# Clustered attention and a rational MoE layer in one kernel: the second head pair's operands turned by TensorE, its row maxima entered in three steps, the constant products on a tile of ones, and a new order of work

## The chip, the cores and the metric

The kernel runs on one core of a Trainium2 chip. The metric is the device time of one execution in microseconds (us). The kernel before takes 903.31 us, the median of three runs (903.31, 903.31, 904.04).

## The reference

What is computed, cut to what matters (batch 4, 8 heads, 768 positions, head dimension 64, 16 centroids per head; 3072 tokens, d_model 512, d_ff 2048):

```python
q_assign = argmax(q_n @ c_n.T); k_assign = argmax(k_n @ c_n.T)   # normalised rows, per head
mask = q_assign[:, :, :, None] == k_assign[:, :, None, :]
scores = where(mask, scale * q @ k.T, -1e9)
attn = exp(scores - max(scores)); attn = attn / (sum(attn) + 1e-9)
x = (attn @ v)                                  # heads side by side: (3072, 512)
h = x @ w_in
P = a[0] + a[1]*h + a[2]*h**2 + a[3]*h**3
Q = 1 + abs(b[0])*abs(h) + abs(b[1])*h**2
out = (P / (Q + 1e-6)) @ w_out
```

## The kernel before

Each of the four batches has an attention part (four pairs of heads) and an MoE part (three blocks of 256 tokens). The attention of batch b+1 runs beside the MoE part of batch b, so that batch 0's attention stands alone at the head of the program, beside the conversion of the weights, and batch 3's MoE part at its end. Operands are split into two f16 parts so that f16 products keep enough bits: `q1`/`k1` hold high and low part side by side, `q2`/`k2` hold a high part, the marks of the clusters (±65504, which make the mask by a product) and, in batch 0, 16 columns for the row maximum.

All of the order is written out by hand: `op(...)` only records a closure, and `Plan.emit` (L52) calls the closures by the list `ORDER` (L61). Each engine takes its instructions strictly in that order. The loads and the transposing DMAs are all issued by SyncE, in one order too, and the raw weights go through two buffers (`wraw`).

Batch 0 takes the path of `KEYMAJOR`. For each pair:

- `prep` loads q and k, sums squares on ScalarE, finds the pair's scale with four small TensorE products (`over_partitions`, L1010 to L1018: `kt`, `kb`, `qt`, `qb`) and small VectorE steps, and makes `q1`, `k1`, `q2`, `k2` (tiles `tq`, `tk`).
- The operands are turned, head dimension on the partitions (tiles `sq`, `sk`). `turn` (L1098) does it with one transposing DMA each. `turn_pe` (L973) does it with 12 TensorE products with the identity (L980) into one of the two PSUM buffers `s`, and two ScalarE copies (L998) out of it. Which one is used is set by `pet`, which holds the pairs of batch 0 that take TensorE: before, pair 0 alone.
- `attend_keys` computes twelve blocks of scores (L1386), and VectorE takes the maximum of each row (L1396, tile `top`). The maxima go into the last columns of `q2` by five small VectorE steps (L1419 to L1442), and those columns have to be turned as well. Where `q2` is split (a pair in `pet`), that is done in three parts, each as soon as its third of the maxima is there: four TensorE products (L1452) and one ScalarE copy (L1459). Where it is not, the five steps run once over all twelve blocks and `q2` is turned a second time by DMA.
- Then the scores are computed again the other way round (L1480), with the maximum and the mask inside the product, and go through `Exp` and the product with v (L1501, L1507).

The program also contains 16 bursts of eight products with a constant tile (`warm`, L781), whose result nobody reads. They read `ident16`, the f16 identity, which VectorE casts from the f32 identity that GpSimd makes (L389, L390).

Of the kernel before, what the change touches and what calls it, by code (L numbers as in the profile page):

```python
# [12 lines left out]
BF16 = mybir.dt.bfloat16  # L13
# [5 lines left out]
P = 128  # L19
# [38 lines left out]
K = {'xn': 14, 'scp': 1, 'vsc': 0.75, 'sup0': 0, 'stk': 2, 'lop': 0, 'mgp': 0, 'rvn': 2, 'at': 3, 'vn': 3, 'ah': 5, 'sua': 1.0, 'T1': 1, 'quick': 1, 'sqd': 0.0, 'gld': 0.0, 'gp': 0.3, 'pp': 0.0, 'NR': 19, 'acb': 1.0, 'warm': 16, 'fast': 16, 'pet': (0,), 'wdl': 0.5}  # L58
# [200 lines left out]
def clustered_attention_moe_kernel(  # L259
# [12 lines left out]
    nc = tc.nc  # L272
# [52 lines left out]
    def kn(name, default=0.0):  # L325
        return K.get(name, default)

# [10 lines left out]

    TOGETHER = kn('together', ())

    KEYMAJOR = {(b, hp) for b in range(B) for hp in range(kn("km", (4, 0, 0, 0))[b])}

    plan.look = kn("look", 40.0)
    NM = 2
# [1509 lines left out]
```

## Time and profile before

| | before |
|---|---|
| median of three runs | 903.31 us |
| profiled execution, its own time | 900.24 us |
| span of its trace | 898.4 us |
| TensorE busy | 862.0 us (96%) |
| VectorE busy | 811.3 us (90%) |
| ScalarE busy | 794.5 us (88%) |
| GpSimd busy | 533.2 us (59%) |

The span is what the trace covers of the profiled execution; 1.84 us of its own time lie around it. Three engines are busy for most of the span, but not in the same stages: which of them sets the pace is read from a table by stage. TensorE's granted clock is 1.00 in all stages from 50 to 880 us and lower in parts of the first 50.

### The profile page before, as it was taken

How to read it: one execution, taken by the hardware profiler on the slowest of the kernel's cores; microseconds unless marked ns; L12 is line 12 of the kernel's file. 1: busy time of each engine (PE TensorE's matmuls, PEld its weight loads, DVE VectorE, ACT ScalarE, POOL GpSimd, SP SyncE). 2: the span in 40 equal slices, each digit the busy share in tenths (PEclk: the TensorE clock that was granted, in tenths of full speed). 3: DMA queues.
4: the chain of work that ended last, by engine and by line, in shares of the span. 5: the costliest groups of instructions: out<-in, count | busy, mean ns of one | idle time of the engine just before them, and what ended most of it. 6: DMA issues, size and time to landing. Idle time of an engine off the chain costs nothing.

```text
span 898.4 us, 20920 instructions
## 1 busy us (share of the span) xinstructions
PE 862.0 (96%) x7893; PEld 594.4 (66%) x7893; DVE 811.3 (90%) x1610; ACT 794.5 (88%) x1497; POOL 533.2 (59%) x530
## 2 busy tenths in 40 slices
PE   5699999988999999999999999999999999999998
PEld 4566777765666666657667666667676666767654
DVE  3999989789999999989999999999999998877793
ACT  4688899999999999999999999999999999895652
POOL 2337645677766385547556737565666555687664
PEclk9799999999999999999999999999999999999999
DMA  4698876779877999886979999989789875150000
GB/s 155 190 251 216 198 186 144 206 146 210 160 139 139 191 198 183 190 161 127 216 153 167 178 189 171 159 169 179 152 154 170 156 139 95 36 95 1 24 24 24
DMA packets 353013, 135.76 MB, mean 151 GB/s; under 512 B 327824, under 2 KB 344208, under 8 KB 352912
## 3 DMA queue, kind: packets, MB, share of 16 engines
q1 hardware_dynamic: 352912, 134.42, 74.0%
q8 instruction: 62, 1.02, 0.4%
q14 instruction: 39, 0.32, 0.1%
HBM read 41.98 MB, written 6.29 MB: 54 GB/s over the span
## 4 chain that ended last, share of the span: by engine, by line
PE 61%; DVE 17%; ACT 14%; issue 5%; POOL 1%; DMA 1%; SPq 1%; ACTq 0%; DVEq 0%
PE po L1761 20%; PE ph L1612 19%; PE s L1243 7%; PE px L1323 5%; DVE s L1272 3%; ACT s L409 3%; DVE ah L1303 3%; ACT u L409 2%; ACT ah L409 2%; PE s L1386 2%; PE z L1480 2%; PE px L1501 2%; DVE t L1637 1%; DVE t L1630 1%; PE ptl L1138 1%
## 5 line engine op out<-in xcount | busy, mean ns | idle before, releaser
L1612 PE MATMUL ph<-x,win 128*128 128x256 f16 x2304 | 266.2, 273 | 1.1 <-DVE t L1637 0.6
L1761 PE MATMUL po<-wout,g 128*128 128x512 f16 x1152 | 267.1, 379 | 0.0
L1612 PEld LDWEIGHTS <-win 128*128 128x128 f16 x2304 | 223.9, 98 | 42.0 <-DVE t L1637 2.9
L1761 PEld LDWEIGHTS <-g 128*128 128x128 f16 x1152 | 110.5, 98 | 120.1 <-issue 3.4
L1750 POOL TENSOR_TENSOR g<-t,u 128x512 f16<-128x512 f32 x84 | 112.7, 1344 | 93.8 <-DVE t L1743 56.6
L1677 POOL TENSOR_TENSOR s<-s,u 128x512 f32<-128x512 f32 x84 | 111.2, 1329 | 74.9 <-ACT s L409 73.1
L1272 DVE TENSOR_SCALAR_CACHE_REDUCE s<-s,cc 128x768 f32<-128x768 f32 x144 | 144.9, 1018 | 4.4 <-PE s L1243 3.5
L1303 DVE SCALAR_TENSOR_TENSOR ah<-s,su,ah 128x768 f16<-128x768 f32 x144 | 144.1, 1010 | 4.4 <-ACT ah L409 3.9
L409 ACT ACTIVATE ah<-s,su 128x768 f16<-128x768 f32 x144 | 127.8, 899 | 6.6 <-DVE su L1291 6.1
L409 ACT ACTIVATE s<-s,nm 128x768 f32<-128x768 f32 x144 | 125.6, 872 | 8.4 <-DVE s L1272 6.5
L1243 PE MATMUL s<-sk,sq 128*128 128x384 f16 x576 | 115.6, 327 | 6.3 <-DVE ah L1303 5.6
L1243 PEld LDWEIGHTS <-sq 128*128 128x128 f16 x576 | 52.0, 98 | 49.9 <-DVE ah L1303 16.4
L1323 PE MATMUL px<-at,vhi 128*64 128x256 f16 x864 | 73.9, 275 | 1.9 <-DVE s L1731 1.8
L409 ACT ACTIVATE t<-ph,gk 128x512 f32<-128x512 f32 x84 | 65.3, 778 | 0.0
L1630 DVE SCALAR_TENSOR_TENSOR t<-ph,gk,t 128x512 f32<-128x512 f32 x84 | 62.2, 742 | 2.5 <-ACT t L409 1.4
L1637 DVE SCALAR_TENSOR_TENSOR t<-t,gk,ph 128x512 f32<-128x512 f32 x84 | 62.3, 741 | 1.2
L409 ACT ACTIVATE u<-s,cq 128x512 f32<-128x512 f32 x84 | 59.8, 721 | 3.0 <-POOL s L1677 2.9
L409 ACT ACTIVATE s<-u,g 128x512 f32<-128x512 f32 x84 | 60.3, 723 | 0.5
L409 ACT ACTIVATE u<-ph,gk 128x512 f32<-128x512 f32 x84 | 57.7, 688 | 3.3 <-PE ph L1612 3.1
L1731 DVE SCALAR_TENSOR_TENSOR s<-s,g 128x512 f32<-128x512 f32 x84 | 59.8, 714 | 0.5
L1323 PE MATMUL px<-at,vlo 128*64 128x256 f16 x432 | 59.7, 273 | 0.0
L1323 PEld LDWEIGHTS <-vhi 128*64 128x64 f16 x864 | 45.0, 110 | 15.3 <-issue 10.3
(241 smaller groups left out, 1552.4 us busy)
## 6 DMA issues: line engine op xcount, KB each, us to landing
rwi<-in_moe_w_in_dram SPq DMA_DIRECT2D x16, 512.0 KB, 3.9
rwo<-in_moe_w_out_dram SPq DMA_DIRECT2D x16, 512.0 KB, 4.3
rk<-in_k_dram SPq DMA_DIRECT2D x32, 192.0 KB, 3.9
rq<-in_q_dram SPq DMA_DIRECT2D x32, 192.0 KB, 3.7
rvm<-in_v_dram SPq DMA_DIRECT2D x16, 384.0 KB, 4.0
rv<-in_v_dram SPq DMA_DIRECT2D x16, 384.0 KB, 4.1
out_dram<-ob SPq DMA_DIRECT2D x24, 256.0 KB, 2.9
sq<-sq SPq DMA_DIRECT2D x12, 192.0 KB, 4.1
```

The source lines that it names most:

```text
L409: lambda: nc.scalar.activation(out=out(), in_=in_(), func=func, **{a: (x() if callable(x) else x) for a, x in kw.items()}),
L1243: nc.tensor.matmul(sc.ap[:, i, :SH], lhsT=st["q" + x].ap[:, j, t, :], rhs=st["k" + x].ap[:, j, ks, :].rearrange("p t c -> p (t c)"), start ...
L1272: lambda nm=nm, view=view: ts(out=view(), in0=view(), scalar1=cc.ap[:, 0:1], scalar2=None, op0=ALU.mult, op1=ALU.min, accum_out=nm.ap),
L1303: lambda part=part, view=view, su=su: stt(out=part(1), in0=view(), scalar=su.ap, in1=part(0), op0=ALU.mult, op1=ALU.subtract),
L1323: nc.tensor.matmul(px.ap[j * D : (j + 1) * D, :], lhsT=vv.ap[:, j, kt, :], rhs=at[j].ap[:, p_, kt].rearrange("p t c -> p (t c)"), start=(i ...
L1612: nc.tensor.matmul(ph.ap[:, fi * TW : (fi + 1) * TW], lhsT=win[:, wpart, c, f * P : (f + 1) * P], rhs=xs[c].ap[:, xpart], start=(i == 0), ...
L1630: lambda t=t, h=h, ph=ph, col=col: stt(out=t[h].ap, in0=ph.ap, scalar=col("rho")(), in1=t[h].ap, op0=ALU.mult, op1=ALU.mult),
L1637: lambda t=t, h=h, ph=ph, col=col: stt(out=t[h].ap, in0=t[h].ap, scalar=col("a1")(), in1=ph.ap, op0=ALU.add, op1=ALU.mult),
L1677: lambda uv=uv, sv=sv: nc.gpsimd.tensor_tensor(out=sv(), in0=sv(), in1=uv(), op=ALU.mult),
L1731: lambda sv=sv, g16=g16: stt(out=sv(), in0=sv(), scalar=1.0 + 1e-6, in1=g16(0), op0=ALU.add, op1=ALU.mult),
L1750: lambda tv=tv, uv=uv, g16=g16, e=(nc.vector if kshare("gld", b, i_) else nc.gpsimd): e.tensor_tensor(out=g16(1), in0=tv(), in1=uv(), op=A ...
L1761: nc.tensor.matmul(po[ti].ap, lhsT=g16(gg)[:, c0 : c0 + P], rhs=wout[:, wpart, f, :], start=(i == 0 and f == 0), stop=(i == 2 and f == NF ...
```

## The change

Three edits of the code and a new `ORDER`:

- `pet` is `(0, 1)`: pair 1 of batch 0 goes through `turn_pe` for `k1`, `q1`, `k2`, `q2`, and its `q2` is split into three parts.
- The constant products of `warm` read a new tile `w16w`, bf16 ones, set by one VectorE memset. `ident16` is made by GpSimd directly and no longer cast by VectorE.
- `KEYMAJOR` is written in another way and holds the same four pairs of batch 0.
- `ORDER` has 4476 entries for 4453, and the entries stand in another order. Below the new memset all line numbers are higher by 3.

```diff
-K = {'xn': 14, ..., 'warm': 16, 'fast': 16, 'pet': (0,), 'wdl': 0.5}
+K = {'xn': 14, ..., 'warm': 16, 'fast': 16, 'pet': (0, 1), 'wdl': 0.5}

 ORDER = [int(i) for i in """
-4438 4450 40 41 42 43 4437 4447 4445 4449 4444 4443 4452 4448 44 3 4 74 75 5 6 76 77 78 79 386 387 389 4451
...

-    KEYMAJOR = {(b, hp) for b in range(B) for hp in range(kn("km", (4, 0, 0, 0))[b])}
+    KEYMAJOR = {(0, hp) for hp in kn("kmset", (0, 1, 2, 3))}

     ident16 = cp.tile([P, P], F16, name="ident16")
-    nc.vector.tensor_copy(out=ident16, in_=ident)
+    make_identity(nc, ident16)
+    w16w = cp.tile([P, P], BF16, name="w16w")
+    nc.vector.memset(w16w, 1.0)

-                nc.tensor.matmul(wm.ap[:, :P], lhsT=ident16, rhs=ident16, start=True, stop=True)
+                nc.tensor.matmul(wm.ap[:, :P], lhsT=w16w, rhs=w16w, start=True, stop=True)
```

By engine, the program has these instructions more or fewer: TensorE 48 turning products and 12 of the rows of maxima more; ScalarE 8 copies of turned tiles and 3 of rows more; VectorE 15 small steps of pair 1 for 5, a memset for a cast; SyncE 5 transposing DMAs fewer (2 of `sk`, 3 of `sq`); GpSimd one memset and one select more for the second identity.

Three places of the order. The first is VectorE's beginning, up to the first step of pair 0's scale (`km`, the maximum of the sums of k's squares; `ww..` are raw weights, `ident` in L390 the f16 identity). Before:

```order
L445 TENSOR_REDUCE css<-csq 128x1
L448 TENSOR_SCALAR cn<-css 128x1
L558 TENSOR_SCALAR wwo_1_222<-mwo_1_218 128x512
L565 SCALAR_TENSOR_TENSOR wwo_1_222<-rwo_1_216,wwo_1_222 128x512
L390 CAST ident_85<-ident 128x128
L1015 TENSOR_REDUCE km_0_245<-kt_0_243 1x1
L1027 TENSOR_SCALAR ksc_0_249<-kb_0_247 128x1
```

Changed:

```order
L388 MEMSET eps 128x1
L393 MEMSET w16w 128x128
L395 MEMSET mrow 128x8
L396 MEMSET mrow 128x8
L397 MEMSET mrow 128x1
L398 MEMSET mrow 128x1
L561 TENSOR_SCALAR wwo_1_149<-mwo_1_147 128x512
L568 SCALAR_TENSOR_TENSOR wwo_1_149<-rwo_1_127,wwo_1_149 128x512
L561 TENSOR_SCALAR wwi_2_232<-mwi_2_228 128x512
L568 SCALAR_TENSOR_TENSOR wwi_2_232<-rwi_2_226,wwi_2_232 128x512
L1018 TENSOR_REDUCE km_0_253<-kt_0_242 1x1
```

What the constant products read is written behind two weight tiles before, and ahead of all weights in the change. TensorE's own order begins with eleven of the bursts and `kt` in both.

The second is ScalarE where pair 1's operands are turned (`sk_1`, `sq_1`; `mwo`, `gwo` are parts of raw weights, `rvm` v for its scale). Before:

```order
L409 ACTIVATE tq_1_455<-rq_1_452,qsc_1_474 128x12x64
L409 ACTIVATE mwo_0_537<-rwo_0_535 128x512
L409 ACTIVATE gwo_0_548<-rwo_0_535 128x512
L998 ACTIVATE sk_0_550<-tk_0_0_485 128x768 x2
L998 ACTIVATE sq_0_553<-tq_0_0_500 128x3x256 x2
L409 ACTIVATE mwo_2_565<-rwo_2_563 128x512
L409 ACTIVATE gwo_2_570<-rwo_2_563 128x512
L409 ACTIVATE mwo_3_580<-rwo_3_578 128x512
L409 ACTIVATE gwo_3_632<-rwo_3_578 128x512
L409 ACTIVATE rvm_1_745,vm_313<-rvm_1_745 128x768
```

Changed:

```order
L1001 ACTIVATE sk_0_554<-tk_0_0_541 128x768 x2
L1001 ACTIVATE sq_0_539<-tq_0_0_526 128x3x256
L412 ACTIVATE mwo_2_599<-rwo_2_597 128x512
L412 ACTIVATE gwo_2_617<-rwo_2_597 128x512
L1001 ACTIVATE sk_1_621<-tk_0_1_584 128x768
L412 ACTIVATE wip_ln<-win_623,tiny 128x1
L1001 ACTIVATE sk_1_621<-tk_0_1_584 128x768
L412 ACTIVATE mwo_3_636<-rwo_3_634 128x512
L412 ACTIVATE gwo_3_641<-rwo_3_634 128x512
L1001 ACTIVATE sq_1_672<-tq_0_1_644 128x768 x2
```

Four of the eight new copies stand between the conversions of the raw weights; the copies of `k2` and `q2` stand 10 and 18 rows further on, among the first exponentials.

The third is SyncE, where pair 1's `k2` and `q2` were turned. Before:

```order
L423 DMA rwi_1_886<-in_moe_w_in_dram 128x1024
L1105 DMA_TRANSPOSE sk_1_896<-tk_1_542 128x12x128
L423 DMA rwi_3_912<-in_moe_w_in_dram 128x1024
L1105 DMA_TRANSPOSE sq_1_981<-tq_1_546 128x12x128
L423 DMA rwi_2_1016<-in_moe_w_in_dram 128x1024
L1105 DMA_TRANSPOSE sk_2_1034<-tk_2_756 128x12x128
```

Changed:

```order
L426 DMA rwi_0_888<-in_moe_w_in_dram 128x1024
L426 DMA rwi_1_960<-in_moe_w_in_dram 128x1024
L426 DMA rwi_2_1018<-in_moe_w_in_dram 128x1024
L426 DMA rk_3_1098<-in_k_dram 128x384
L1108 DMA_TRANSPOSE sk_2_1100<-tk_2_730 128x12x128
L426 DMA rwi_3_1112<-in_moe_w_in_dram 128x1024
```

The transposing DMAs of pair 1 are gone from between the loads; those of pair 2 follow.

## Rows read from the trace of the kernel before

**Rows 1.** Busy time by stage: stretch, its length, engines (us, instructions), granted clock, DMA share.

```profile
9.20:15.70 6.50, 6.49 (x88) 6.50 (x89) 0.00 (x0) 1.24 (x5) 2.98 (x4) 1.00 0.28 91
15.70:20.00 4.30, 2.31 (x27) 1.63 (x25) 2.75 (x12) 2.62 (x5) 0.00 (x0) 0.94 0.02 4
20.00:35.00 15.00, 10.35 (x120) 9.24 (x121) 14.02 (x42) 12.42 (x21) 3.77 (x4) 0.61 0.58 187
35.00:50.00 15.00, 12.69 (x135) 8.56 (x134) 14.34 (x29) 7.45 (x15) 6.75 (x7) 0.84 0.92 245
50.00:100.00 50.00, 48.50 (x527) 33.41 (x526) 48.50 (x113) 43.56 (x77) 29.06 (x30) 1.00 0.90 218
100.00:125.00 25.00, 24.47 (x340) 18.37 (x342) 20.48 (x45) 22.81 (x42) 12.62 (x13) 1.00 0.96 209
125.00:175.00 50.00, 49.14 (x637) 36.77 (x627) 43.81 (x102) 46.97 (x89) 30.89 (x37) 1.00 0.66 172
175.00:225.00 50.00, 44.13 (x469) 32.19 (x465) 46.57 (x99) 49.26 (x100) 34.42 (x43) 1.00 0.88 178
225.00:450.00 225.00, 220.21 (x1949) 148.75 (x1948) 218.39 (x432) 218.56 (x428) 138.51 (x132) 1.00 0.89 170
450.00:700.00 250.00, 249.84 (x2219) 171.48 (x2218) 245.95 (x497) 242.81 (x468) 148.91 (x145) 1.00 0.90 165
```

**Rows 2.** Timeline, 1 to 18 us: start, length, engine, instruction [idle before <- releaser].

```profile
1.14 0.06 DVE L387 MEMSET eps<- 128x1 f32 x1
...
8.93 0.22 DVE L390 CAST ident<-ident 128x128 f16<-128x128 f32 x1
9.02 0.19 ACT L409 ACTIVATION_READ_ACCUMULATOR tk<-rk 128x1 f32 x1
9.21 1.03 PE L786 MATMUL warm-39.99_113<-ident 128*128 128x128 f16 x8 [9.21 <-DVE ident L390]
...
15.30 0.61 PE L786 MATMUL warm-39.86_234<-ident 128*128 128x128 f16 x8
15.75 0.27 PE L1013 MATMUL kt<-ident,sumk 128*1 128x128 f32 x1
16.05 0.28 DVE L1015 TENSOR_REDUCE km<-kt 1x1 f32<-1x128 f32 x1 [6.90 <-PE kt L1013]
...
17.38 0.94 ACT L409 ACTIVATE tk<-rk,ksc 128x768 f16<-128x768 f32 x1 [6.87 <-DVE ksc L1045]
```

**Rows 3.** VectorE groups by line and shape, 0 to 215 us: count | busy us, mean ns.

```profile
L1442 DVE TENSOR_SCALAR tq<-rest 128x12 f16<-128x12 f32 x3 | 1.0, 344 | 0.1
L1419 DVE TENSOR_SCALAR tq<-top 128x32 f16<-128x32 f32 x3 | 0.5, 178 | 0.1
L1437 DVE SCALAR_TENSOR_TENSOR rest<-tq,rest 128x12 f32<-128x12 f16 x3 | 0.5, 170 | 0.1
L1427 DVE SCALAR_TENSOR_TENSOR rest<-tq,top 128x4 f32<-128x4 f16 x3 | 0.5, 151 | 0.0
```

**Rows 4.** All groups by line and shape: TensorE's turning and ScalarE's copies of pair 0.

```profile
L998 ACT ACTIVATE sq<-tq 128x768 f16<-128x768 f16 x4 | 3.0, 818 | 0.0
L998 ACT ACTIVATE sk<-tk 128x768 f16<-128x768 f16 x4 | 3.0, 806 | 0.4 <-PE tk L980 0.4
L980 PE MATMUL tk<-ident,tk 128*128 128x128 f16 x24 | 2.9, 310 | 3.0 <-DVE tk L1181 1.8 <-DVE tk L1089 1.2
L1459 ACT ACTIVATE sq<-r 32x512 f16<-32x512 f16 x3 | 1.8, 589 | 0.8 <-PE r L1452 0.7
L1452 PE MATMUL r<-ident,tq 128*32 128x128 f16 x12 | 1.2, 222 | 0.0
```

**Rows 5.** Busy time in one stretch in which TensorE turns pair 0's `k2`; columns as in rows 1.

```profile
31.60:32.90 1.30, 1.28 (x13) 1.30 (x14) 1.26 (x3) 1.30 (x3) 0.00 (x0) 0.50 0.05 13
```

**Rows 6.** Line L1105 from 45 to 125 us: who waited for a transposing DMA (us, times).

```profile
  POOL tq L1127: 0.4, 1
  PEld L1138: 0.2, 1
```

More of the change, by code (lines that the diff above doesn't have):

```diff
@@ L55, in emit @@
             self.ops[i]()
-K = {'xn': 14, 'scp': 1, 'vsc': 0.75, 'sup0': 0, 'stk': 2, 'lop': 0, 'mgp': 0, 'rvn': 2, 'at': 3, 'vn': 3, 'ah': 5, 'sua': 1.0, 'T1': 1, 'quick': 1, 'sqd': 0.0, 'gld': 0.0, 'gp': 0.3, 'pp': 0.0, 'NR': 19, 'acb': 1.0, 'warm': 16, 'fast': 16, 'pet': (0,), 'wdl': 0.5}
+K = {'xn': 14, 'scp': 1, 'vsc': 0.75, 'sup0': 0, 'stk': 2, 'lop': 0, 'mgp': 0, 'rvn': 2, 'at': 3, 'vn': 3, 'ah': 5, 'sua': 1.0, 'T1': 1, 'quick': 1, 'sqd': 0.0, 'gld': 0.0, 'gp': 0.3, 'pp': 0.0, 'NR': 19, 'acb': 1.0, 'warm': 16, 'fast': 16, 'pet': (0, 1), 'wdl': 0.5}
 ORDER = [int(i) for i in """
[193 rows of a table removed]
[194 rows of a table added]
 """.split()]
```

386 rows, old and new, of the table ORDER are left out of this document.

## The prediction

> **What bounds the kernel now.** I read first the busy time by stage, then the timeline of the first 18 us, then the groups of the instructions that the change multiplies, and last who waits for a transposing DMA.
>
> The stages show which engine sets the pace [rows 1]. From 450 to 700 us TensorE is busy 249.84 of 250 us: there only less work for it, or an earlier start, can shorten the kernel. From 20 to 100 us VectorE is the fullest engine (14.02 of 15, 14.34 of 15, 48.50 of 50), with TensorE level with it after 50. From 125 to 225 ScalarE is (46.97 and 49.26 of 50), and TensorE's largest hole lies at the end of that, 5.87 us between 175 and 225; another 4.79 are spread over 225 to 450. Before 20 us no engine is full. From 9.20 to 15.70 VectorE is busy for 0.00 us and ScalarE for 1.24: TensorE runs the constant products, and all else waits.
>
> The timeline shows why [rows 2]. The constant products need the f16 identity; its cast is the 19th row of VectorE's order and starts at 8.93 us, behind two weight tiles that come by DMA. So the first burst starts at 9.21. The sum of k's squares is ready at 9.21 (9.02 plus 0.19), but `kt`, the product that takes it, stands behind eleven bursts in TensorE's order and starts at 15.75. VectorE's `km` has then waited 6.90 us, and ScalarE's next step on k, which starts at 17.38, 6.87 us. This is a chain at the head of a program whose later stages are full, so what it loses is lost at the end, unless something later has slack of its own.
>
> **The change part by part.**
>
> *The constant tile.* The ones are set right behind `eps`, which is set at 1.14 us, and depend on nothing. The eleven bursts take 6.5 us (9.21 to 15.75), so they end near 8 us, before the sums are there, and `kt` starts at about 9.2: 6.5 us earlier. If each burst took the 1.03 us of the first, they would end at 12.6 and 3.1 us would be left. I take -6.5, with -3.1 as the other end. What is late next is the scale's own chain (`km` to 17.38: 1.3 us of small steps in turn on VectorE and TensorE), which moves as a whole. The second identity costs GpSimd two instructions, which I put at 0: they stand ahead of nothing that is waited for, since GpSimd is idle for more than half of 9.20 to 20 us and the identity is needed only when turning begins. The cast that VectorE loses is paid by the memset, 0.
>
> *The small steps of the maxima.* Pair 1 has 15 for 5. The short ones take 151 to 178 ns, the long ones 170 to 344 [rows 3]: 2.3 to 2.7 us for 0.9 to 1.7, thus +0.6 to +1.9. VectorE is full where they stand, so they lie on the path: +1.2. The maxima that they read, behind which they queue, are made in the same order as before.
>
> *TensorE's turning.* 24 products took 2.9 us, 121 ns each [rows 4]; they ran at a granted clock of 0.50, the 1.2 GHz level [rows 5], and half of that is the least at 2.4 GHz. 48 are 2.9 to 5.8 us. The 12 of the maxima's rows are 1.2. The first 24 stand before and among the first scores, where TensorE is idle for 4.65 and 2.31 us of two stages of 15 [rows 1], and so cost nothing; if that cover is gone, 2.9. The other 24 and the rows, 1.5 + 1.2 = 2.7, fall where it has only 1.50 us idle in 50. I take +1.2, between 0 and 7.0.
>
> *ScalarE's copies.* Eight copies at 3.0/4 = 0.75 us and three at 0.59 [rows 4] are 7.8 us. They queue ahead of weight conversions and of the first exponentials. ScalarE is idle for 7.55 us between 35 and 50 and for 6.44 between 50 and 100 [rows 1], and VectorE, not ScalarE, is full there: 0. If that cover is gone, up to 7.8.
>
> *Five transposing DMAs less.* Only 0.6 us of waiting ended on such a DMA between 45 and 125 us [rows 6], and the loads that they stood between come sooner on SyncE's queue: -0.6 to 0, I take 0. The DMA engines are at 0.92 and 0.90 from 35 to 100 [rows 1], so this is room rather than time.
>
> *The new order.* What it does to the later holes no row of before tells. The bounds are the largest hole that it could fill or open again, 5.9 us either way; I take 0, since in both orders each engine has nearly the same work ahead of the first MoE product.
>
> The sum: -6.5 + 1.2 + 1.2 = -4.1 us. The profiled execution took 900.24, its span and 1.84 around it, which gives 896.1. The median of the runs stands 3.07 above the profiled execution, so on that scale **899.2 us**. A measurement of this kernel can tell about 0.2% from no change, 1.8 us: faster is under 901.5, slower is over 905.1.
>
> **The rivals.**
>
> *The order also fills the hole of 175 to 225.* Pair 1 done earlier would let ScalarE, full there, come to the first MoE blocks sooner. For it: the 5.87 us [rows 1]. Against it: ScalarE gets 7.8 us more to do ahead of that stage. 899.2 - 5.9 = 893.3. Chance 0.17.
>
> *The early start is half swallowed by the loads.* From 35 us on the DMA engines are nearly full, and the raw weights pass through two buffers. If the stages from there on come no sooner than their loads, half of the 6.5 is lost: 899.2 + 3.3 = 902.5, no change that can be told. Against it: the DMA engines are at 0.28 and 0.02 while everything waits for `kt` [rows 1], so loads can move up too. Chance 0.15.
>
> *ScalarE takes over.* A turned operand holds one of the two PSUM buffers that the scores need until ScalarE has copied it, and the copies queue behind weight conversions, which wait for loads. If ScalarE's idle time from 35 to 50 is such waiting and comes back in another place, all copies lie on the path: -6.5 + 1.2 + 7.8 = +2.5, 905.8, slower. It decides from 2.4 us of copies that find no idle time (-6.5 + 2.4 = -4.1): beyond that ScalarE's path is the longest of the three engines'. Against it: VectorE is the full one there. Chance 0.12.
>
> *TensorE stays at the lower clock.* It is granted 0.50 while it turns `k2` although it is busy for 1.28 of 1.30 us [rows 5], 0.61 over 20 to 35 us and 0.84 over 35 to 50 [rows 1]. The change puts more turning there, with the products for the weights' squares but no constant burst right before the first scores. If the clock were 0.50 over the whole stretch of 35 to 50, TensorE's 12.69 us would become 12.69 x 0.84/0.50 = 21.3, 6.3 more than the 15 there are: -4.1 + 6.3 = +2.2, 905.5, slower. Against it: VectorE's maxima pace these scores in any case. Chance 0.11. The Trainium skill, "TensorE: Matmul & The Clock Gate", Part 4 (PE-mode transpose), has a rule that speaks for this one: turning products don't count as activity for the clock gate as others do, so that the full clock does not come on by them. By that rule this rival would hold and the time be 905.5; the row agrees with it, but by the row alone the clock could as well be low from the idle time ahead of the turning, and 899.2 stand.
>
> **How the numbers follow.** The forecast has 0.45 and lies within 896.5 to 901.5 by the bounds of the two small terms and of a start of -5 to -6.5. With the first rival that is 0.62 on the fast side, of which I leave 0.02 for its edge: faster 0.60. No change is the second rival with parts of the edges, 0.22. Slower is 0.18, most of the last two. The range leaves out the far part of the first rival (0.06) and most of the cases above 905 (0.13): 893.0 to 905.0.
>
> **What would show it.** The start is right if the first burst begins before 2 us and `kt` at 9.2 to 9.7, with `km`'s wait of 6.90 gone. The cover is right if ScalarE stays under VectorE's share up to 100 us, and the first maxima come 5 to 6 us earlier. If the turning costs what I say, TensorE's busy time after 50 us grows by under 4 us. The end should come 4 us earlier with the idle time of 175 to 450 as before (10.7 us). It is wrong if `kt` still waits, if TensorE's clock stays at 0.50 through the scores, or if that idle time moves by more than 4 us.

## The result and the profile after

The changed kernel takes 894.92 us, the median of 4 runs (892.88 to 895.60), beside 903.54 (903.31 to 904.04) for the kernel before in the same comparison: ratio 0.990, 95% interval 0.9882 to 0.9918. By the ratio that is 9.0 us less (7.4 to 10.7), and 8.6 between the two medians. It is faster, as forecast, and inside the range, but by more than twice the 4.1 us of the sum. The profiled execution took 895.56 us with a span of 893.8, which is 4.7 less than that of before; why this smaller number is not the effect is shown by the first experiment.

Busy time by stage, which answers to [rows 1] (same columns):

```profile
9.20:15.70 6.50, 4.61 (x52) 3.84 (x51) 5.13 (x22) 4.64 (x10) 1.39 (x2) 0.86 0.51 162
20.00:35.00 15.00, 10.13 (x93) 8.58 (x94) 14.63 (x33) 12.66 (x23) 8.66 (x9) 0.77 0.59 185
35.00:50.00 15.00, 13.94 (x161) 10.20 (x160) 13.75 (x41) 12.12 (x23) 5.32 (x6) 1.00 0.54 168
50.00:100.00 50.00, 48.20 (x538) 33.83 (x537) 47.92 (x109) 43.11 (x78) 25.80 (x25) 1.00 0.72 190
175.00:225.00 50.00, 44.74 (x415) 32.36 (x415) 44.92 (x93) 47.07 (x94) 33.78 (x44) 0.93 0.75 148
225.00:300.00 75.00, 74.90 (x672) 51.41 (x670) 73.70 (x145) 74.82 (x151) 50.40 (x46) 1.00 0.91 173
225.00:450.00 225.00, 222.58 (x1962) 150.85 (x1959) 220.67 (x440) 221.06 (x437) 135.33 (x129) 1.00 0.92 174
```

From 9.20 to 15.70 VectorE is busy for 5.13 us instead of 0.00. From 35 to 50 TensorE's clock is 1.00 instead of 0.84 and ScalarE has 12.12 us of work instead of 7.45. From 225 to 450 TensorE is idle for 2.42 us instead of 4.79. From 175 to 225 it is idle for 5.26 instead of 5.87, but at a granted clock of 0.93 instead of 1.00.

The timeline of the first 18 us, which answers to [rows 2]:

```profile
1.18 0.17 DVE L393 MEMSET w16w<- 128x128 bf16 x1
1.40 1.03 PE L789 MATMUL warm-39.97_118<-w16w 128*128 128x128 bf16 x8 [1.40 <-DVE mrow L395]
...
8.99 0.27 PE L1016 MATMUL kt<-ident,sumk 128*1 128x128 f32 x1
9.30 0.28 DVE L1018 TENSOR_REDUCE km<-kt 1x1 f32<-1x128 f32 x1 [1.64 <-PE kt L1016]
...
11.03 0.94 ACT L412 ACTIVATE tk<-rk,ksc 128x768 f16<-128x768 f32 x1 [2.23 <-DVE ksc L1048]
```

The first burst starts at 1.40 instead of 9.21, `kt` at 8.99 instead of 15.75, and `km`'s wait of 6.90 is 1.64.

ScalarE's copies, by line and shape, which answer to [rows 4]:

```profile
L1001 ACT ACTIVATE sq<-tq 128x768 f16<-128x768 f16 x8 | 6.2, 805 | 0.2 <-PE tq L983 0.2
L1001 ACT ACTIVATE sk<-tk 128x768 f16<-128x768 f16 x8 | 6.2, 812 | 0.6 <-PE tk L983 0.6
L1462 ACT ACTIVATE sq<-r 32x512 f16<-32x512 f16 x6 | 3.5, 590 | 2.4 <-PE r L1455 2.3
```

Two of TensorE's turnings, `k2` of pair 0 and then `k2` of pair 1:

```profile
25.94 1.49 PE L983 MATMUL tk<-ident,tk 128*128 128x128 f16 x12
43.50 0.83 PE L983 MATMUL tk<-ident,tk 128*128 128x128 f16 x12
```

The work came as sized: a copy takes 0.78 us (0.75 forecast), a copy of rows 0.58 (0.59), and each of pair 1's four turnings 0.83 or 0.84 us, 3.3 in all (2.9 to 5.8). What it did to the waits is another matter.

### The profile page after: what moved, and what is told of

It reads as the page before. It is cut to its first block, busy times and chain, and to the rows that moved or that the text cites. A ratio compares the mean times of both kernels' runs of the same rounds, so it can differ in the third digit from the quotient of the medians.

```text
span 893.8 us, 21071 instructions
## 1 busy us (share of the span) xinstructions
PE 867.1 (97%) x7953; PEld 601.0 (67%) x7953; DVE 808.8 (90%) x1620; ACT 801.4 (90%) x1508; POOL 530.7 (59%) x532
## 4 chain that ended last, share of the span: by engine, by line
PE 63%; DVE 19%; ACT 10%; issue 4%; POOL 1%; DMA 0%; SPq 0%; ACTq 0%; DVEq 0%; POOLq 0%
PE po L1764 21%; PE ph L1615 19%; PE s L1246 7%; PE px L1326 5%; DVE s L1275 4%; DVE ah L1306 3%; PE px L1504 2%; PE s L1389 2%; ACT s L412 2%; PE z L1483 2%; PE px L1510 1%; DVE t L1640 1%; DVE s L1734 1%; ACT u L412 1%; DVE t L1633 1%
## 5 line engine op out<-in xcount | busy, mean ns | idle before, releaser
L1753 POOL TENSOR_TENSOR g<-t,u 128x512 f16<-128x512 f32 x84 | 115.3, 1377 | 89.0 <-DVE t L1746 54.4
L1680 POOL TENSOR_TENSOR s<-s,u 128x512 f32<-128x512 f32 x84 | 113.4, 1357 | 70.9 <-ACT s L412 69.3
```

What stands on the lines that cost most here:

```text
L1680: lambda uv=uv, sv=sv: nc.gpsimd.tensor_tensor(out=sv(), in0=sv(), in1=uv(), op=ALU.mult),
L1753: lambda tv=tv, uv=uv, g16=g16, e=(nc.vector if kshare("gld", b, i_) else nc.gpsimd): e.tensor_tensor(out=g16(1), in0=tv(), in1=uv(), op=A ...
```

## The experiments

Each kernel is compared with the kernel before on its own chip; a ratio is turned into us by 902 us. Line numbers in rows are those of the kernel in question and shift by a few.

**How much two executions of one kernel differ.** The kernel before, with no edit.

> The kernel before, unchanged, as a measure of how far its executions differ among themselves. Its profiled execution took 900.24 us and its timed runs 903.31 to 904.04. If the profiled one was an exception, the executions here lie at 903 to 904 with spans near 901.5, and the profile shows where some 3 us more are lost than in the first trace. If the kernel before has a real spread of 3 us, executions at 900 to 901 come up among these too.

Measured: 902.40 us (900.53 to 903.98, 12 runs), ratio 1.0008 (0.9998 to 1.0018); the runs of before on that chip lie between 899.62 and 904.24 (23 runs). So single executions differ by over 4 us, and the profiled one of the prediction, 900.24, is near the lower end. The second trace (span 902.2) has its first maximum 0.9 us later, its first MoE product 1.6 later, and loses 2.0 more at once near 395 us. The trace of before in that stretch:

```profile
390.00:395.00 5.00, 5.00 (x30) 2.35 (x25) 4.20 (x9) 4.64 (x10) 0.39 (x2) 1.00 1.14 211
```

and the second one:

```profile
390.00:395.00 5.00, 5.00 (x38) 2.63 (x34) 1.96 (x3) 1.26 (x4) 1.72 (x2) 0.66 1.16 232
```

TensorE comes out of an idle time shortly before (1.79 us in the first, 2.19 in the second); in the second the granted clock is then 0.66, and VectorE and ScalarE are busy there for 1.96 and 1.26 of 5 us. What follows: 3.07 us between the median and the profiled execution were the luck of one execution and no scale for the other kernel. The 4.7 us between the two profiled executions understate the change, because that of before lies below its median (900.24 against 903.54) and that of the change above its own (895.56 against 894.92).

**The ones alone.** The kernel before with two edits:

```diff
+    w16w = cp.tile([P, P], BF16, name="w16w")
+    nc.vector.memset(w16w, 1.0)
-                nc.tensor.matmul(wm.ap[:, :P], lhsT=ident16, rhs=ident16, start=True, stop=True)
+                nc.tensor.matmul(wm.ap[:, :P], lhsT=w16w, rhs=w16w, start=True, stop=True)
```

> The kernel before with nothing but the ones: the constant products read a tile of ones that is set at about 1.2 us. Theory (the early start is handed on): kt starts at 9.0 to 9.5 us instead of 15.75, all maxima come 6 to 7 us earlier, and the time is 897 us (896 to 899). Rival (the loads or the later stages swallow the start): the first score comes earlier, but the first product of the MoE part by less than 3 us, and the time is 900 to 903.

Measured: 896.32 us (894.88 to 896.92), ratio 0.9941 (0.9927 to 0.9955), 5.3 us less. Its trace is that of before, moved as a whole: `kt` 6.4 us earlier, the 48 maxima of batch 0 (twelve for each pair) 6.4 to 7.6, the first MoE product 6.6, the last product 5.5. The early start is handed on through every stage.

**All but the ones.** The change, with its constant products reading the cast identity:

```diff
-    make_identity(nc, ident16)
-    w16w = cp.tile([P, P], BF16, name="w16w")
-    nc.vector.memset(w16w, 1.0)
+    nc.vector.tensor_copy(out=ident16, in_=ident)
-                nc.tensor.matmul(wm.ap[:, :P], lhsT=w16w, rhs=w16w, start=True, stop=True)
+                nc.tensor.matmul(wm.ap[:, :P], lhsT=ident16, rhs=ident16, start=True, stop=True)
```

> The changed kernel with the constant products reading the cast identity again, as before. Theory (the start is what the change gains): kt again near 15.7 us and the time 900 to 902. Rival (the new order and pair 1's turning bring the gain and the start only moves idle time about): under 898.

Measured: 899.17 us (896.79 to 903.92, 12 runs), ratio 0.9972 (0.9955 to 0.9990), 2.5 us less (0.9 to 4.1). This lies between the theory's 900 to 902 and the rival's 898 and decides for neither as it stands: the start is not all of the gain, and turning, small steps and order together gain too, where +2.4 was forecast. With the ones this makes 7.8, and the change, run once more on another chip, has 0.991, or 8.1: the two parts add up.

**Pair 1 turned in the old places.** The ones, `pet` as in the change, and the old `ORDER` with each new instruction where the one that it replaces had stood:

```diff
-K = {..., 'pet': (0,), 'wdl': 0.5}
+K = {..., 'pet': (0, 1), 'wdl': 0.5}
```

> e1_ones with pair 1's operands turned by TensorE and its maxima entered in three steps, each new instruction in the place where the old one stood; all other work in the order of the kernel before. Theory (the edit costs what it adds and gains nothing by itself): 1 to 3 us over e1_ones. Rival (transposing DMAs out of the way is a gain of its own): at or under e1_ones. If ScalarE takes over, 4 us or more over e1_ones.

Measured: 907.93 us (907.35 to 909.97), ratio 1.0074 (1.0060 to 1.0088): slower than before, and 11.6 us slower than with the ones alone. That is far from the theory's 1 to 3 and in the range that was named for ScalarE taking over, 4 or more. The waits between 30 and 50 us (who <- for whom: us, times, longest):

```profile
ACT sk L993 <- PE tk L975: 4.2, 1, 4.2
DVE mx L1147 <- PE ptl L1133: 3.4, 1, 3.4
PE ptl L1133 <- ACT sq L993: 1.1, 2, 0.9
PE tq L975 <- DVE top L1391: 0.9, 1, 0.9
```

and the timeline, 36 to 44 us:

```profile
37.73 0.83 PE L975 MATMUL tk<-ident,tk 128*128 128x128 f16 x12
38.60 1.51 ACT L993 ACTIVATE sk<-tk 128x768 f16<-128x768 f16 x2 [4.19 <-PE tk L975]
39.46 0.83 PE L975 MATMUL tq<-ident,tq 128*128 128x128 f16 x12 [0.90 <-DVE top L1391]
...
40.33 1.51 ACT L993 ACTIVATE sq<-tq 128x768 f16<-128x768 f16 x2 [0.22 <-PE tq L975]
41.20 0.47 PE L1133 MATMUL ptl<-cen,sq 128*128 128x16 f16 x12 [0.90 <-ACT sq L993]
...
43.06 0.56 DVE L1147 TENSOR_REDUCE mx<-ptl 128x24 f32<-128x384 f32 x1 [3.37 <-PE ptl L1133]
```

Products, two copies, products, two copies, and then the products that read both stand in a row on TensorE, with no score between them. So VectorE has no block to reduce from 39.7 to 43.1 us. Its busy time and the clock of that stage:

```profile
35.00:50.00 15.00, 11.36 (x119) 7.61 (x117) 8.99 (x21) 6.97 (x14) 6.13 (x7) 0.77 0.67 219
```

8.99 us against 13.75 in the change. Against the ones alone, 6.2 us are lost between the 4th and the 8th maximum, 3.7 more up to the 16th and 3.1 up to the 32nd. The rows above are about the first of these losses; what the other two wait for stays open.

**The same work in other places, by hand.** Only the four turnings of pair 1 and their copies are moved. On ScalarE:

```diff
-L404 ACTIVATE gwo_3_634<-rwo_3_580 128x512
-L993 ACTIVATE sk_1_650<-tk_0_1_637 128x768 x2
-L993 ACTIVATE sq_1_666<-tq_0_1_653 128x768 x2
+L993 ACTIVATE sk_1_658<-tk_0_1_606 128x768 x2
+L404 ACTIVATE gwo_3_663<-rwo_3_580 128x512
+L993 ACTIVATE sq_1_665<-tq_0_1_629 128x768 x2
```

> The kernel before with the ones tile and pair 1 turned by TensorE in the old order (907.93, ratio 1.0074), with only the four turnings and their eight copies moved: k1's products before four of pair 0's scores and its copies behind them, q1's products between these scores, k2's and q2's some places earlier, among the scores and exponentials, each copy behind other work of ScalarE. Same instructions, same work. Theory 'place': the 11.6 us come from products, copies and scores that wait for each other in turn; most of it comes back: ratio 0.994 to 0.999 (897 to 901 us), and the jump of 6.3 us between maxima 3 and 7 falls to under 2. Theory 'work': TensorE's and ScalarE's added work lies on the path wherever it stands: ratio 1.005 or more (905 to 908).

Measured: 905.57 us (903.13 to 907.81), ratio 1.0033 (1.0019 to 1.0047). In the traces the 8th maximum comes 3.1 us earlier, the 24th 3.7, the end 1.6. The jump between the 4th and the 8th falls to 0.6 us, as 'place' said, but 2.8 us are now lost between the 2nd and the 3rd. There the scores wait until ScalarE has copied `sq` out of the PSUM buffer:

```profile
PE s L1381 <- ACT sq L993: 1.6, 1, 1.6
```

So the place matters, but the ratio lies in the range of neither theory: by it four moves give back 3.7 us of some 12, not most of them.

**Which part of the order.** Two orders, called hybrids below, are put together from two halves, with the seam behind operation 430 (pair 1's last score). The first has the change's order up to there, then the old one with pair 1 turned:

```diff
+order = changed[:430] + [i for i in old_places if i not in set(changed[:430])]
```

> The first 430 operations in the change's order (through the last score of pair 1), all others in the old order; everything else as in the change, but that the constant identity comes by a cast. Theory 'head': what the order is worth (some 12 us against the old places) is won by the places around the two turned pairs alone: ratio 0.988 to 0.994, the maxima within 1 us of the change's. Theory 'whole order': the later order holds a part of it: ratio 0.997 or more.

and the reverse:

```diff
+order = old_places[:430] + [i for i in changed if i not in set(old_places[:430])]
```

> The reverse: the first 430 operations in the old order with pair 1 turned by TensorE in the old places, all others in the change's order. Theory 'head': the maxima stand 10 to 12 us later than in the change and nothing makes that good: ratio 1.003 to 1.009 (905 to 910). Theory 'whole order': the later order gives back some of it: ratio 0.995 to 1.001.

Measured: 908.37 us, ratio 1.0065 (1.0052 to 1.0079), and 918.40, ratio 1.0176 (1.0159 to 1.0193). By its number the first fits 'whole order', the second fits neither. The trace of the first shows another cause: up to 76 us it runs within 0.1 us of the change, 8.2 us ahead of the old places (24th maximum), and then loses 14.7 us. SyncE's queue there:

```profile
73.28 0.77 SPq L418 DMA_DIRECT2D rwo<-in_moe_w_out_dram  x1
89.29 0.38 SPq L418 DMA_DIRECT2D rv<-in_v_dram  x1
89.86 0.33 SPq L418 DMA_DIRECT2D rwo<-in_moe_w_out_dram  x1
90.76 1.43 SPq L418 DMA_DIRECT2D rwi<-in_moe_w_in_dram  x1
```

SyncE issues nothing from 74.1 to 89.3 us: the load of pair 2's v (`rv`) waits 15.2 us until TensorE has read the last of an earlier v, and the weight loads stand behind it. ScalarE then has no work from 84.7 to 95.2 us, VectorE from 86.8 to 96.0 and TensorE from 91.5 to 97.3:

```profile
75.00:100.00 25.00, 16.41 (x175) 9.94 (x174) 15.11 (x36) 12.94 (x24) 10.66 (x11) 0.85 0.25 86
```

The seam had put that load too early; in the second hybrid it is pair 1's v, for 19.5 us.

**One load moved.** In the first hybrid `rv` of pair 2 goes behind six weight loads (three by the expectation), in the second that of pair 1 behind three:

```diff
-L418 DMA rv_2_1424<-in_v_dram 128x2x384
...
+L418 DMA rv_2_1910<-in_v_dram 128x2x384
```

> As the run with the change's order up to operation 430 and the old order behind it (908.37, ratio 1.0065), but one load is moved: that of pair 2's v goes on SyncE's queue behind three weight loads and some transposing DMAs, about where the change has it. In that run it stood ahead of them, waited 15.2 us for its buffer, and everything stood 13.9 to 14.7 us later from 93 us on. Theory 'one load': the 14 us are this wait; ratio 0.989 to 0.994 (893 to 897), no jump between maxima 23 and 31, and the order's worth is all in its first 430 operations. Theory 'whole order': half or more stays, ratio 0.997 or more.

> As the run with the old order up to operation 430 and the change's order behind it (918.4, ratio 1.0176), but the load of the second half of pair 1's v goes back to its old place, behind three weight loads, on SyncE's queue; there it stood ahead of them and waited 19.5 us. Theory 'one load': the 13 us between maxima 23 and 31 go, ratio 1.002 to 1.007 (904 to 909), as with pair 1 turned in the old places throughout: the later order alone gives nothing. Theory 'whole order': it falls below that, to 0.997 to 1.001, because the later order wins back time. If neither moves it from 1.015, the load is not the cause.

Measured: 899.05 us (896.79 to 901.87, 12 runs), ratio 0.9969 (0.9958 to 0.9980), and 911.48, ratio 1.0101 (1.0086 to 1.0116). In the traces the 32nd maximum comes 9.5 and 9.8 us earlier, the end 12.0 and 7.7. In the first:

```profile
75.00:100.00 25.00, 21.61 (x234) 14.79 (x233) 22.01 (x46) 19.05 (x32) 14.03 (x14) 0.93 0.44 136
```

Between the medians it is 9.3 and 6.9 us: that much one load in the wrong place of one queue cost. But both miss the numbers of theory 'one load': the first is behind the change by 5.2 us at the 32nd maximum, 4.1 at the first MoE product and 3.3 at the end, and the second (1.0101) is not faster than the old places throughout (1.0074). Against those places the head of the order, with this load moved, gives back 9.5 us by the ratio, about two thirds of what the whole order does; the tail alone gives nothing that shows in the time.

**The low clock after 185 us.** The change once more, unchanged:

> The changed kernel once more, unchanged, on the chip of the three kernels below. If its gain is the sum of the ones tile (ratio 0.9941, measured alone) and of the rest (0.9972), the ratio to the kernel before is 0.989 to 0.992. The trace also tells whether the low granted clock from 185 to 215 us (0.71 to 0.84 in the first trace) belongs to this order (rival A: it comes back, and with it 2 to 3 us between the first MoE product and the end) or to that one execution (rival B: clock 1.00 there, span 2 to 3 us shorter than 893.8).

Measured: 894.41 us (892.81 to 895.85), ratio 0.991 (0.9895 to 0.9926). The trace agrees with the first within 0.3 us from end to end, the low clock with it:

```profile
182.50:185.00 2.50, 1.70 (x37) 1.60 (x38) 2.26 (x7) 2.02 (x8) 0.89 (x3) 0.99 0.70 238
185.00:187.50 2.50, 2.50 (x34) 1.93 (x31) 2.37 (x6) 2.50 (x6) 0.00 (x0) 0.50 0.03 8
187.50:190.00 2.50, 2.50 (x20) 1.91 (x18) 1.80 (x6) 0.95 (x3) 0.00 (x0) 0.83 0.00 0
```

TensorE waits in short pieces for three small results (0.32, 0.37 and 0.71 us), and then runs the first MoE products at 0.50, the 1.2 GHz level; at 187.5 ScalarE runs out of work (0.95 of 2.5). Filled with constant products:

```diff
-            def spread(px=px, rq=rq):
+            def spread(px=px, rq=rq, tb=tb):
+                if n == "0_3" and tb == 2:
+                    for _ in range(12):
+                        nc.tensor.matmul(px.ap[:, 1, :P], lhsT=w16w, rhs=w16w, start=True, stop=True)
```

> The change with 12 constant products more, into the part of a PSUM tile that the next product overwrites, at 183 us: there TensorE waits 0.71 us for VectorE, and the first MoE products behind it run at a granted clock of 0.50 from 185.0 to 187.5 and 0.83 to 190. Theory 'clock': with the wait filled the clock stays at 1.00, the first MoE products take half as long, and all from 190 us on stands 1.0 to 2.5 us earlier (span 891.5 to 893, against 893.8 and 894.1 in two executions). Theory 'elsewhere': the clock falls all the same, or ScalarE and VectorE set the pace there; the end moves by less than 0.5 us.

Measured: 892.83 us (892.60 to 893.90), ratio 0.9897 (0.9883 to 0.9912). The trace (span 892.1):

```profile
182.50:185.00 2.50, 2.50 (x62) 2.35 (x63) 2.29 (x6) 2.02 (x8) 0.63 (x2) 1.00 0.57 199
185.00:187.50 2.50, 2.50 (x33) 2.24 (x30) 2.40 (x7) 2.50 (x6) 0.00 (x0) 1.00 0.02 7
187.50:190.00 2.50, 2.50 (x24) 2.05 (x22) 2.10 (x5) 2.38 (x5) 0.00 (x0) 1.00 0.00 0
205.00:207.50 2.50, 1.67 (x24) 1.59 (x26) 2.38 (x7) 2.50 (x7) 2.35 (x4) 0.85 0.10 22
207.50:210.00 2.50, 2.50 (x19) 1.38 (x16) 2.50 (x5) 2.47 (x5) 1.14 (x1) 0.50 1.02 195
210.00:212.50 2.50, 2.50 (x17) 1.39 (x15) 1.57 (x3) 2.50 (x5) 0.00 (x0) 0.97 0.99 225
```

The clock stays at 1.00. The 48th MoE product starts 1.8 us earlier than in the trace above; 0.4 of that is there at the first MoE product, so 1.4 us lie between the two (1.3 against the first trace of the change). The trace fits theory 'clock', but the traces together do not prove it. In the second hybrid before its load was moved, TensorE has the same three waits (0.33, 0.37 and 0.73 us) with nothing filled in, and the clock stays at 1.00 all the same:

```profile
207.87:210.37 2.50, 1.66 (x36) 1.57 (x37) 2.26 (x7) 2.00 (x8) 0.93 (x3) 1.00 0.52 182
210.37:212.87 2.50, 2.50 (x44) 2.29 (x41) 2.40 (x6) 2.50 (x6) 0.00 (x0) 1.00 0.04 7
```

With these waits left as they are, the clock fell in three traces (the change twice, the second hybrid with its load moved) and stayed up in this one; with the last of them filled it stayed up in both traces that there are, this one and the next. What the filling is worth in the time is not shown either: the ratios (0.9897 and 0.991) do not tell this version from the change, whose two traced executions lie at or near the top of their runs (895.56 of 892.88 to 895.60, 895.85 of 892.81 to 895.85).

**The second dip.** The rows from 205 us on show another, near 208 us. There TensorE waited for a PSUM tile that VectorE reads late, so two VectorE steps were moved ahead of two others (operations 982 and 983 ahead of 941 and 942):

```diff
-... 1477 ... 941 942 982 983
+... 1477 982 983 ... 941 942
```

> The change with the 12 constant products at 183 us, and with two of VectorE's steps (the 0.75 us steps that read the PSUM tile of the third MoE block's first products) moved ahead of two other steps of 0.69 and 0.75 us. In the run with the constant products alone TensorE waited 1.99 us at 203.8 us for the second of these steps, and then ran at a granted clock of 0.50 to 0.85 from 205 to 210. Theory 'path': the wait falls to about 0.5 us, the clock stays at 0.95 or more, and all behind stands 1.0 to 2.0 us earlier (span 890 to 891 against 892.1). Theory 'VectorE and ScalarE set the pace there' (2.4 and 2.5 of 2.5 us busy): TensorE's products come earlier, but the end moves by less than 0.5 us, or up to 0.7 later for the two steps put back.

Measured: 895.10 us (894.13 to 895.18), ratio 0.9914 (0.9900 to 0.9928), span 893.3. TensorE's wait fell from 2.0 to 0.6 us and the clock stayed up, but the end came 1.2 us later, 0.2 of it there at the first MoE product. Neither theory allowed for that much:

```profile
205.00:207.50 2.50, 2.38 (x37) 1.69 (x34) 2.37 (x7) 2.50 (x7) 1.36 (x2) 1.00 0.04 9
207.50:210.00 2.50, 1.83 (x8) 0.68 (x9) 2.50 (x5) 1.36 (x3) 2.35 (x3) 1.00 1.01 192
210.00:212.50 2.50, 1.12 (x7) 0.67 (x7) 2.50 (x5) 1.65 (x3) 0.81 (x1) 1.00 0.93 235
```

VectorE is full (2.37, 2.50, 2.50) and the steps put back delayed what ScalarE needs (1.36 and 1.65 of 2.5 instead of 2.47 and 2.50). This says that the reordering cost more than the clock gave back, not that the low clock there is free: the run took away both at once.

## Why the prediction was right and wrong

- **The start (-6.5): right.** The first burst starts at 1.40 and `kt` at 8.99, a little before the 9.2 to 9.7 that was named; of `km`'s wait of 6.90, 1.64 are left. Alone it gives 5.3 us by the ratio (4.1 to 6.6) and 5.5 in the trace. The rival in which the loads swallow half of it fell: with the ones alone the trace moves as a whole. The signs of the cover came as well, ScalarE under VectorE's share from 20 to 100 us and the first six maxima 5.3 to 8.3 us earlier (5 to 6 forecast), but they did not tell what the chain costs without the new order.
- **Small steps, turning and copies (+1.2, +1.2, 0): the step that failed.** They were costed as work against the idle time of stages, and the work had the size that was forecast. What counts is the chain: turned tile, PSUM buffer, copy, reader, on engines that take their work in order. In the old places it costs 11.6 us; only the far ends of the bounds (1.9, 7.0, 7.8) hold that, not the values taken. It is akin to the rival in which ScalarE's copies hold the buffers, but not the same: in the trace the copies stand behind no weight conversion; ScalarE waits 4.19 us for TensorE's products, which stand behind pair 0's scores. The change pays less for the chain. How much less is known only for the head of its order with one load moved (9.5 us given back); parting the turnings by hand gave 3.7, so which other moves count is not shown.
- **The new order (0): the other step that failed.** That "in both orders each engine has nearly the same work" says nothing of waits. With pair 1 turned and the ones in both, the old places have 907.93 and the change's order 894.41 and 894.92: the order is worth some 13 us (15 by the ratios). Terms and order together were put at +2.4 and gave -2.5. That is where the sum went wrong, and the start, which gave 1.2 us less than forecast, hides a part of it.
- **Where the net gain lies.** Not ahead of the MoE part: there the change has gained 5.1 us at the first MoE product, less than the ones alone (6.6). TensorE's idle time from 225 to 450, 4.79 us in [rows 1], is 2.42 in the change. The stretch of 225 to 300 alone, in the trace of before,

```profile
225.00:300.00 75.00, 73.37 (x647) 49.46 (x646) 73.38 (x141) 73.87 (x147) 48.78 (x44) 1.00 0.83 149
```

and with the ones alone,

```profile
225.00:300.00 75.00, 73.28 (x667) 49.58 (x667) 73.65 (x144) 73.15 (x145) 46.05 (x41) 1.00 0.82 152
```

  has 1.63 and 1.72 us of idle time, and 0.10 in the change (above). The hybrids tell which part of the order closes it. The same 75 us, counted from 40 us behind the first MoE product, in the hybrid with the head of the change's order and the old order behind it, and in the one with the old head and the change's order behind it (each with its load moved):

```profile
229.42:304.42 75.00, 73.27 (x664) 49.80 (x663) 73.47 (x143) 73.75 (x149) 45.60 (x41) 1.00 0.81 155
241.62:316.62 75.00, 74.90 (x672) 51.42 (x670) 73.65 (x143) 74.81 (x150) 50.89 (x45) 1.00 0.89 173
```

  The first has 1.73 us of idle time, the second 0.10. Counted so, it is 1.63 to 1.74 in the traces of all seven kernels and repetitions with the old order behind operation 430, and 0.00 to 0.10 in all seven with the change's. So the later order closes this hole. The rival that the order fills a hole had the right kind of gain, but named 175 to 225, where 5.26 of 5.87 remain. The prediction's test, the end 4 us earlier "with the idle time of 175 to 450 as before (10.7 us)", answers the same way: the idle time is 7.68.
- **The scale (+3.07): wrong.** The spread of executions made it; without it the same sum would have said 896.1, and 1.2 us would have been missed instead of 4.3. That nearness would have been luck: terms that missed by 4.9 against a trace of before that was some 3 us short. The band of 896.5 to 901.5 that the forecast was given does not follow from its own bounds either: with 903.31, -6.5 + 0.6 + 0 is 897.4 and -5 + 1.9 + 7.0 is 907.2.
- **The lower clock while turning: did not come.** The granted clock is 0.77 and 1.00 in the two stages of 15 us that were 0.61 and 0.84. Pair 0's last two turnings still run at 0.50 (1.49 us each), pair 1's four at 1.00 (0.83 or 0.84). The rule of the Trainium skill, "TensorE: Matmul & The Clock Gate", Part 4 (PE-mode transpose), that turning products don't count as activity for the clock gate as others do, is neither shown nor refuted: scores lie between pair 1's turnings here. Where the clock did fall, in the old places (0.77 from 35 to 50), TensorE was idle for 3.64 of 15 us.

What stays open: which moves of the head avoid the chain's waits, which moves of the later order close the hole, and how many us the later order is worth by itself, since the seam of the hybrids costs time of its own.

## What to carry to other kernels

Work moved from a queue to an in-order engine is not priced by the idle time there, but by the chain through its buffers: here the same work cost 11.6 us in one order and was more than made good in another, so judge it together with its order. Before a predicted scale is taken from one profiled execution, look at how far executions of the same kernel differ. The same holds for two traces that are compared: a small difference between them counts when other traces repeat it. A wait of a load for its buffer is a wait of every load behind it on the same queue (15.2 us here).

## What was not expected of the hardware

- One load that waits 15.2 us for its buffer at the head of SyncE's queue left three engines without work; moving that one load gave back 9.5 us at the 32nd maximum and 9.3 between the medians.
- Waits of 0.3, 0.4 and 0.7 us in a row on TensorE were followed by the granted clock of 0.50 in three traces, and by 1.00 in a fourth with the same waits. With 12 constant products in the last of them it stayed at 1.00 in two traces; in the first of these the products behind came 1.3 to 1.4 us sooner. The old order shows the same uncertainty: behind one wait of 1.36 us the first 48 MoE products take 5.8 us with the ones alone, and 7.0 us, at 0.50 for a part of them, in the first hybrid before its load was moved.
- One kernel's executions differ by 4.6 us (899.62 to 904.24). Between two traces of it 2.0 us arise at one place, where the clock after an idle time is 0.66 in one execution and 1.00 in the other.
